# Attention into a gated MLP: two loads brought forward on the DMA queue, and one transposition moved to another PSUM bank

## The chip, the cores and the metric

The kernel runs on one core of a Trainium2 chip. The metric is device time in microseconds for one execution. The engines named below are TensorE (PE, with its weight loads as PEld), VectorE (DVE), ScalarE (ACT), GpSimd (POOL) and SyncE (SP). POOL and SP also issue DMA transfers.

## The reference

```python
# q, k, v: (8, 12, 448, 64); x: (3584, 768); w_gate, w_val: (768, 1536); w_out: (1536, 768)
scores = scale * np.matmul(q, k.transpose(0, 1, 3, 2))
attn = np.exp(scores - max); attn = attn / (sum + 1e-09)
attn_out = np.matmul(attn, v)
x = attn_out.transpose(0, 2, 1, 3).reshape(B * S, H * D)
g = x @ w_gate
silu = g * (1.0 / (1.0 + np.exp(-g)))
return (silu * (x @ w_val)) @ w_out
```

Eight sequences of 448 positions and twelve heads go through softmax attention; the joined heads go through a gated MLP. Inputs and output are float32.

## The kernel before

**Tiles.** The 96 heads are worked on as 48 pairs, six pairs to a sequence. The 3,584 tokens of the MLP are eight blocks of alternately 384 and 512 tokens (`block`, L573). In the MLP, `ffn1_steps` (L488) makes the gate and value products (L493) of one 128-wide slice of the hidden dimension, applies tanh on ACT (L511) and two products on DVE (t at L516, hts at L519); `ffn2_steps` (L526) multiplies by the output weights (L544) and stores through ACT (L551). The output weights are two halves of columns, wo 0 and wo 1 (1,152 KB each in fp16). The first block does all its steps with wo 0 before those with wo 1.

**Attention of one pair.** Keys and queries are loaded with a cast to fp16 on POOL's DMA queue (`load_qk16`, L144, queries at L157; from pair 12 on the keys come as two transfers, one for each half of the partitions, at L138). From pair 14 on a buffer of two pairs is filled by two calls: the even pair of the two takes the buffer, the odd one fills its other half. Then the pair is turned so that the head dimension lies on the partitions. Pairs 1 to 10 are turned by TensorE (`turn`, L249, transposes at L258, copied out by DVE at L259). Pair 11 (L217 copies on POOL, transposes on SP's queue at L220 and L224) and all pairs from 12 on (L194, then L196 and L200) are turned by DMA transposes, which need POOL's copies first; the copies write one of three buffers in turn (tag qk16). The scores (L299 up to pair 11, from 12 on L268 and, for the leftover rows of two pairs together, L281) are followed by the exponential on ACT (L307, L289) and the product with V (L325, L333, L362). V comes by POOL's queue too (L168, from pair 12 on L138) and is copied beside a column of ones by DVE (L175).

**PSUM.** Six of the eight banks are three score banks of two, taken in turn by `stile` (L115) through the list `sring`. The other two are the pool `ps_f`, taken in turn by the value product, the output product, the attention accumulators, the turns and, where `gate_small` is set, a gate product. A user waits until the reader of the same bank before it has ended.

**Order.** The order of work is written out by hand: the program order of each engine is the order in which the Python code emits it. Pairs 0 to 5, with the scores of pair 6's first two chunks, follow the string `order` (L682). After that a loop over `plan` (L739) makes visits x = 0, 1, 2, ... Visit 0 has pair 6's chunks 0 and 1 (already scored), visit 1 chunks 2 and 3, visits 2 and 3 pair 7, and from visit 4 on there are three chunks to a visit: pair 8's first chunk is in visit 4, pair 9's in visit 5, pair 10's in visit 6, pair 11's in visit 8, pair 12's in visit 9. A visit scores its chunks, prepares later pairs, does the products with V of finished pairs, and runs a share of the MLP.

**Loads.** Loads are emitted from the table `wq` (L602): entry n is emitted with the second score chunk of pair n in the prologue (L691, pairs 0 to 6) or at the end of the visit that pair n enters (L777). Items are "qk" (first pair, number of calls' pairs; two if left out), "V" (three pairs), "g" and "v" (a quarter of the gate or value weights), and "o" (a half of the output weights). In addition, when pair n enters a visit, `prep` is emitted for pair n + 3 or n + 4 (L755; pair 11 in visit 4, pairs 12 and 13 in visit 5, pair 14 in visit 6, pair 15 in visit 8), then the keys and queries of pair n + LA with LA = 6 (L759), then V of pair n + 3 from pair 12 on (L761). Before the change, visit 4 therefore loads pair 14, visit 5 pair 15, V of pair 12 and, by entry 9 of the table, wo 1. Entry 6 (V of pairs 9 to 11, and wo 0) is emitted in the prologue, with the second chunk of pair 6.

Of the kernel before, what the change touches and what calls it, by code (L numbers as in the profile page):

```python
# [20 lines left out]
LA = 6  # L21
RB = 5
FIRST = 6
# [14 lines left out]
def kernel(  # L38
# [19 lines left out]
    NPAIR = B * NHP  # L58
# [56 lines left out]
    def stile():  # L115
        sring.append(sring.pop(0))
        return sbanks[sring[-1]]

    def dummy(n, w=512):
        wp = ps_f.tile([128, 512], FP32, tag="f", name="wp")  # L120
        for _ in range(n):
            nc.tensor.matmul(wp[:, 0:w], lhsT=warm[:, 0:128], rhs=warm[:, 0:w], start=True, stop=True)
# [67 lines left out]
    def prep_quad(pr):  # L190
        rq, rk = raw[pr]
        qk16 = attp.tile([128, 2, NC, 2, D], FP16, tag="qk16", name="qk16", bufs=3)
        for dst, src in ((qk16[:, 0], rk), (qk16[0:P, 1], rq)):
            nc.gpsimd.tensor_copy(dst.rearrange("p c h d -> p h c d"), src)  # L194
        qkT[pr] = attp.tile([128, NC * 128 + S], FP16, tag="qkT", name="qkT", bufs=QB)
        nc.sync.dma_start_transpose(  # L196
            qkT[pr][:, 0 : NC * 128].rearrange("p (c q) -> p c q", q=128),
            qk16[:, 0].rearrange("p c h d -> p (c h d)"),
        )
        nc.sync.dma_start_transpose(  # L200
            qkT[pr][:, NC * 128 :].rearrange("p (c q) -> p c q", q=P),
            qk16[0:P, 1].rearrange("p c h d -> p (c h d)"),
        )

    def prep(pr):
        if pr >= QUAD:
            return prep_quad(pr)
        rq, rk = raw[pr]
        if pr == 0 or pr >= NPE:
            qk16 = attp.tile([128, 2, NC, 2, D], FP16, tag="qk16", name="qk16", bufs=3)[0:P]  # L210
            for t, src in enumerate((rq, rk)):
                dst = qk16[:, 1 - t].rearrange("p c h d -> p h c d")
                if pr == 0:
                    nc.vector.tensor_copy(dst[:, 0], src[:, 0])
                    nc.scalar.activation(dst[:, 1], src[:, 1], AF.Copy)
                else:
                    nc.gpsimd.tensor_copy(dst, src)  # L217
        qkT[pr] = attp.tile([128, 2 * S + D], FP16, tag="qkT", name="qkT", bufs=QB)
        if pr >= NPE:
            nc.sync.dma_start_transpose(  # L220
                qkT[pr][:, 0 : 2 * S].rearrange("p (c q) -> p c q", q=P),
                qk16.rearrange("p t c h d -> p (t c h d)"),
            )
            nc.sync.dma_start_transpose(  # L224
                qkT[pr][:, 2 * S :].rearrange("p (c q) -> p c q", c=1),
                qk16[0:D, 1, 0].rearrange("p h d -> p (h d)"),
            )
            return None

        def turn0():  # L230
            for t in range(2):
                tp = stile()
                for c in range(NC):
                    for hx in range(2):
                        nc.tensor.matmul(
                            tp[ts(hx, 64), c // 2, ds(c % 2 * P, P)],
                            lhsT=qk16[:, 1 - t, c, hx],
                            rhs=ident[0:P, 0:P],
                            start=True,
                            stop=True,  # L240
                        )
                dst = qkT[pr][:, ts(1 - t, S)].rearrange("p (a x) -> p a x", a=2)
                nc.vector.tensor_copy(dst[:, 0], tp[:, 0, 0 : 2 * P])
                nc.scalar.activation(dst[:, 1], tp[:, 1, 0 : 2 * P], AF.Copy)
                if t == 0:
                    dummy(1, 256)
                    nc.vector.tensor_copy(qkT[pr][:, 2 * S :], tp[:, 0, 0:D])

        def turn():  # L249
            if pr < FIRST + 2:  # L250
                tp = stile()[:, 0].bitcast(FP16)
            else:
                tp = ps_f.tile([128, 1024], FP16, tag="f", name="tp")
            for i in range(2 * NC + 1):
                t, c = (1 - i // NC, i % NC) if i < 2 * NC else (0, 0)
                for hx in range(2):
                    src = raw[pr][t][:, hx, c, :]
                    nc.tensor.transpose(tp[ts(hx, 64), ts(i, P)], src, ident[0:P, 0:P])  # L258
            nc.vector.tensor_copy(qkT[pr][:], tp[:, 0 : 2 * S + D])  # L259

        return turn if pr else turn0
# [31 lines left out]
    def qk(pr, c):  # L293
        if pr >= QUAD:
            return qk_quad(pr, c)
        t = qkT[pr]
        s = stile()
        for hx in range(2):
            nc.tensor.matmul(  # L299
                s[:, hx, 0:S],  # L300
                lhsT=t[ts(hx, 64), c * P : c * P + 128],
                rhs=t[ts(hx, 64), ds(S + (1 - hx) * D, S)],
                start=True,
                stop=True,
            )
        e = Es[pr % NE][:, ds(c * EB, 16)].rearrange("p (h b) x -> p h (b x)", h=2)
        nc.scalar.activation(e[:, :, 0:S], s[0:P, :, 0:S], AF.Exp, scale=sm_scale)  # L307
# [271 lines left out]
    with tc.manual_schedule():  # L579
# [5 lines left out]
        for vo in Vts:  # L585
# [18 lines left out]
            1: [("V", 2), ("qk", 8, 1), ("g", 1), ("v", 1)],  # L604
            3: [("qk", 9, 1), ("qk", 10), ("g", 2), ("v", 2)],
            4: [("g", 3), ("v", 3), ("qk", 12)],
            6: [("V", 3), ("o", 0)],
            9: [("o", 1)],
        }

        def emit(item):
# [127 lines left out]
        for x, (chunks, todo) in enumerate(plan):  # L739
            quads = [u for u in chunks if u[0] >= QUAD and u[1] == RU]  # L740
            for pr, c in quads + [u for u in chunks if u not in quads]:
                if x > 0:
                    qk(pr, c)
            for _, p0 in todo:
                if p0 >= QUAD:
                    pv_piece(p0, RU)
            end = min([y for y in adds if y > x] + [len(plan) + 1])
            if x == 0:
                add_block(0, end)
            early = [p0 for p0 in vcopies.get(x, []) if p0 < QUAD]  # L750
            for p0 in early:
                copy_v(p0)
            entered = [pr for pr, c in chunks if c == 0]
            for pr in entered:
                lead = [pr + 3] if pr + 3 < QUAD else [pr + 3, pr + 4] if pr + 3 == QUAD else [pr + 4]  # L755
                for p in lead:
                    if NPE <= p < NPAIR:
                        prep(p)
                if 14 <= pr + LA < NPAIR:  # L759
                    load_qk16(pr + LA, 1)  # L760
                if 12 <= pr + 3 < NPAIR:  # L761
                    load_v(pr + 3)
            for pr, c in chunks:
                if c == 2 and pr < NPE - 2:
                    prep(pr + 2)()
            if x in adds and x > 0:
                add_block(adds[x], end - x, x)
            for _, p0 in todo:
                pv(p0)
                if p0 < XPE:  # L770
                    turns.append(p0)
                else:
                    turn_x(p0)
            for p0 in vcopies.get(x, []):
                if p0 not in early:
                    copy_v(p0)
            for pr in entered:  # L777
                for w in wq.pop(pr, []):
                    emit(w)
            bare = not todo and bool(chunks)  # L780
            if x == 0:
                carry = left() / end
                for fb in range(3):
                    gate_small[0] = fb == 2
                    carry -= run_fv()
            elif adds[max(y for y in adds if y <= x)] < 2:
                if bare and oq and not fvq:
                    carry -= run_o()
                elif bare:
                    gate_small[0] = True  # L790
                carry = run_budget(left() / (end - x) + carry)
            else:
                nf, no = steps.pop(0) if steps else (0, 0)
                if bare and no:
                    run_o()
                    no -= 1
                elif bare:
                    gate_small[0] = True
                for y in range(nf):
                    if fvq:  # L800
                        run_fv()
                for _ in range(no):
                    run_o()
            if x == 1:
                turn_rests(0)
            while turns:
                turn_x(turns.pop(0))
            if XPE - 1 in [p0 for _, p0 in todo]:
                turn_rests(1)
# [39 lines left out]
```

## Time and profile before

| what | value |
|---|---|
| median of 3 runs | 453.12 us (452.09 to 453.83) |
| the profiled execution | 452.5 us |
| its span (first to last instruction) | 450.7 us |
| mean granted TensorE clock | 0.995 |
| POOL's DMA queue (q0) | 46,832 packets, 24.56 MB, 48.7% of 16 engines' span |
| SP's DMA queue (q1: transposes and stores) | 61,520 packets, 24.66 MB, 28.7% |
| wo, two issues | 1,152 KB each, 14.3 us from issue to landing (median) |

The profile counts the time of an engine's instructions as busy and gives, for every idle stretch, the instruction or transfer that ended it. Times in the trace are microseconds from the start of the span. Sizes of loads are those written (fp16). "Landing" is the time from the issue of a transfer to its completion.

### The profile page before, as it was taken

Reading aid. Unit: us, or ns where it says so; the run is one execution under the profiler, and the core shown is the slowest. Engines: PE = TensorE matmul, PEld = TensorE weight load, DVE = VectorE, ACT = ScalarE, POOL = GpSimd, SP = SyncE. Lnnn points to the kernel's source line nnn. Section 1 sums busy time; section 2 is a strip of 40 time slices with the busy share of each in tenths; the row PEclk is TensorE's granted clock in tenths of the full one; section 3 lists DMA queues with packets and bytes.
Section 4 is the critical chain, followed back from the end, with each engine's and each line's share of the span. In section 5 each row is a group of like instructions: output and inputs, shape, how many; then the busy total and the mean of one; then the engine's idle time right before and its main releaser. Section 6 shows DMA issues by size and latency. Waiting matters only on the chain.

```text
span 450.7 us, 10033 instructions
## 1 busy us (share of the span) xinstructions
PE 438.9 (97%) x4025; PEld 246.7 (55%) x4025; DVE 199.9 (44%) x447; ACT 225.0 (50%) x332; POOL 180.4 (40%) x299
## 2 busy tenths in 40 slices
PE   8999998999999999999999999999999999999996
PEld 3665664544456566554556556554455656644464
DVE  4756551365564344343454434344444434045400
ACT  6975765546553654455536365455454651222222
POOL 8655735997875364336461366423000000000000
PEclk9999999899999999999999999999999999999999
DMA  9999999999997699975975688945131211200033
GB/s 140 176 200 201 197 172 174 154 201 160 134 142 94 108 140 120 125 119 69 125 109 101 111 128 106 155 78 97 32 79 47 50 43 23 79 27 0 0 107 105
DMA packets 108494, 49.90 MB, mean 111 GB/s; under 512 B 60832, under 2 KB 104992, under 8 KB 108448
## 3 DMA queue, kind: packets, MB, share of 16 engines
q0 software_dynamic: 46832, 24.56, 48.7%
q1 hardware_dynamic: 61520, 24.66, 28.7%
q8 instruction: 31, 0.51, 0.5%
q14 instruction: 15, 0.12, 0.1%
q10 hardware_dynamic: 96, 0.05, 0.0%
HBM read 49.55 MB, written 11.01 MB: 134 GB/s over the span
## 4 chain that ended last, share of the span: by engine, by line
PE 78%; DMA 14%; DVE 3%; POOL 2%; issue 1%; ACT 1%; DVEq 0%; ACTq 0%; POOLq 0%
PE op L544 23%; PE s L493 21%; PE vp L493 19%; PE acc L362 8%; DMA wv<-in_moe_w_val_dram 5%; PE s L268 4%; DMA k<-in_k_dram 3%; DMA wo<-in_moe_w_out_dram 3%; DMA wg<-in_moe_w_gate_dram 2%; DVE hts L519 1%; DVE t L516 1%; ACT sg L511 1%; PE s L281 1%; DMA vraw<-in_v_dram 1%; POOL k L157 1%
## 5 line engine op out<-in xcount | busy, mean ns | idle before, releaser
L493 PE MATMUL vp<-X,wv 128*128 128x512 f16 (+1 forms) x564 | 122.4, 353 | 0.1
L544 PE MATMUL op<-wo,hts 128*128 128x384 f16 (+1 forms) x684 | 116.6, 325 | 2.6 <-DMA wo<-in_moe_w_out_dram 2.2
L493 PE MATMUL s<-X,wg 128*128 128x512 f16 (+1 forms) x534 | 116.4, 354 | 0.0
L289 ACT ACTIVATE E<-s 128x896 f16<-128x896 f32 x126 | 106.5, 921 | 13.6 <-PE s L268 8.7
L516 DVE SCALAR_TENSOR_TENSOR t<-sg,s 128x512 f32<-128x512 f32 (+1 forms) x91 | 56.7, 623 | 107.3 <-ACT sg L511 107.3
L511 ACT ACTIVATE sg<-s 128x512 f32<-128x512 f32 (+1 forms) x91 | 49.9, 549 | 93.6 <-PE s L493 91.1
L544 PEld LDWEIGHTS <-hts 128*128 128x128 f16 x684 | 66.1, 98 | 48.3 <-issue 2.9
L493 PEld LDWEIGHTS <-wv 128*128 128x128 f16 x564 | 55.1, 98 | 52.1 <-issue 0.4
L551 ACT ACTIVATE osb<-op 128x384 f32<-128x384 f32 (+1 forms) x57 | 27.7, 486 | 103.7 <-PE op L544 102.3
L493 PEld LDWEIGHTS <-wg 128*128 128x128 f16 x564 | 52.4, 98 | 44.9 <-issue 0.7
L519 DVE SCALAR_TENSOR_TENSOR hts<-t,vp 128x512 f16<-128x512 f32 (+1 forms) x94 | 58.5, 622 | 10.2 <-DVE t L516 0.5
L194 POOL COPY qk<-k 128x512 f16<-128x512 f16 x36 | 22.8, 632 | 99.3 <-DMA qkT<-qk 97.5
L138 POOL DMA_DIRECT2D vraw<-in_v_dram x72 | 43.8, 627 | 9.8 <-DMA wo<-in_moe_w_out_dram 6.5
L138 POOL DMA_DIRECT2D k<-in_k_dram x70 | 42.3, 616 | 7.0 <-DMA wo<-in_moe_w_out_dram 4.8
L362 PEld LDWEIGHTS <-E 128*128 128x128 f16 (+1 forms) x1152 | 37.2, 96 | 13.1 <-issue 7.6
L307 ACT ACTIVATE E<-s 112x896 f16<-112x896 f32 x48 | 40.7, 917 | 6.6 <-PE s L299 5.8
L403 DVE RECIPROCAL R<-acc 128x4 f32<-128x4 f32 x68 | 12.0, 177 | 70.9 <-PE acc L362 70.9
L362 PE MATMUL acc<-vo,E 128*128 128x65 f16 (+1 forms) x1088 | 40.8, 193 | 2.2 <-DVE hts L519 1.9
L157 POOL DMA_DIRECT2D q<-in_q_dram x44 | 30.1, 683 | 5.3 <-PE acc L333 1.8
L404 DVE TENSOR_TENSOR xt<-acc,R 128x256 f16<-128x256 f32 x68 | 28.8, 424 | 2.3
L268 PE MATMUL s<-qkT 64*128 64x448 f16 x216 | 28.3, 355 | 0.0
L194 POOL COPY qk<-q 112x512 f16<-112x512 f16 x36 | 23.1, 642 | 0.0
(70 smaller groups left out, 208.6 us busy)
## 6 DMA issues: line engine op xcount, KB each, us to landing
vraw<-in_v_dram POOLq DMA_DIRECT2D x72, 64.0 KB, 4.5
q<-in_q_dram POOLq DMA_DIRECT2D x41, 112.0 KB, 3.8
k<-in_k_dram POOLq DMA_DIRECT2D x68, 64.0 KB, 4.5
wg<-in_moe_w_gate_dram POOLq DMA_DIRECT2D x8, 288.0 KB, 9.8
wv<-in_moe_w_val_dram POOLq DMA_DIRECT2D x8, 288.0 KB, 10.2
wo<-in_moe_w_out_dram POOLq DMA_DIRECT2D x2, 1152.0 KB, 14.3
out_dram<-osb SPq DMA_DIRECT2D x8, 288.0 KB, 3.7
out_dram<-osb SPq DMA_DIRECT2D x6, 336.0 KB, 2.8
```

The lines of the kernel that those rows point to most:

```text
L138: eng.dma_start(dst[ts(s, 64)], rows)
L157: nc.gpsimd.dma_start(dst[0:P, ds(h0, 2 * n)], flat.rearrange("h (p c) d -> p h (c d)", c=NC))
L194: nc.gpsimd.tensor_copy(dst.rearrange("p c h d -> p h c d"), src)
L268: nc.tensor.matmul(s[:, hx, 0:S], lhsT=t[ts(hx, 64), ts(c + low(pr, hx), 128)], rhs=t[ts(hx, 64), ds(NC * 128, S)], start=True, stop=True,)
L289: nc.scalar.activation(e[:, 0 : 2 * S].rearrange("p (h q) -> p h q", h=2), s[:, :, 0:S], AF.Exp, scale=sm_scale)
L307: nc.scalar.activation(e[:, :, 0:S], s[0:P, :, 0:S], AF.Exp, scale=sm_scale)
L362: nc.tensor.matmul(accs[pr][0][hx][:, ts(j, D + 1)], lhsT=e[rows, ds(hx * S + j * 128, 128)], rhs=Vts[pr % NV][rows, hx, col, 0 : D + 1], ...
L493: nc.tensor.matmul(dst[:, 0:n], lhsT=wslice(kind, fb, cb), rhs=X[kk][:, cb, ds(c0, n)], start=(cb == 0), stop=(cb == NCB - 1),)
L511: nc.scalar.activation(sg[:, 0:n], gp[:, 0:n], AF.Tanh, scale=0.5)
L516: nc.vector.scalar_tensor_tensor(t1[:, 0:n], sg[:, 0:n], 1.0, gp[:, 0:n], ALU.add, ALU.mult)
L519: nc.vector.scalar_tensor_tensor(hts[:, fb, 0:n], t1[:, 0:n], 0.5 * HS, vp[:, 0:n], ALU.mult, ALU.mult)
L544: nc.tensor.matmul(op[:, 0:w], lhsT=hts[:, fb, ts(ch, 128)], rhs=wo[oh][:, fb, ds(m0 - oh * OH, w)], start=(fb == 0), stop=(fb == NFB - 1),)
```

## The change

Three edits. Pair 14's keys and queries are loaded by entry 6 of the table, between V of pairs 9 to 11 and wo 0, instead of in visit 4; the loop over visits loads by itself only from pair 15 on. wo 1 is emitted by entry 7, in visit 2, instead of entry 9, in visit 5; on POOL, which has no other instruction between, it follows wo 0 directly. And pair 8, which was turned in a `ps_f` bank, is turned in a score bank, as pairs 1 to 7 are.

```diff
@@ def turn() in prep
-            if pr < FIRST + 2:
+            if pr < FIRST + 3:
                 tp = stile()[:, 0].bitcast(FP16)
             else:
                 tp = ps_f.tile([128, 1024], FP16, tag="f", name="tp")
@@ the table wq
             4: [("g", 3), ("v", 3), ("qk", 12)],
-            6: [("V", 3), ("o", 0)],
-            9: [("o", 1)],
+            6: [("V", 3), ("qk", 14, 1), ("o", 0)],
+            7: [("o", 1)],
@@ the loop over visits
-                if 14 <= pr + LA < NPAIR:
+                if 15 <= pr + LA < NPAIR:
                     load_qk16(pr + LA, 1)
```

FIRST is 6.

## The prediction

> **What bounds the kernel now.** I read the engine row first, then who TensorE (PE) waited for, then the region of the longest wait: clock, instructions in order of time, and the DMA issues with their landings. PE is busy for 438.9 of the 450.7 us. Its end is the kernel's end, so a microsecond changes the time only if PE idles less or runs at a better clock.
>
> ```profile
> span 450.7 us, 10033 instructions
> PE 438.9 (97%) x4025; PEld 246.7 (55%) x4025; DVE 199.9 (44%) x447; ACT 225.0 (50%) x332; POOL 180.4 (40%) x299
> PE op L544 <- DMA wo<-in_moe_w_out_dram: 2.2, 1, 2.2
> PE tp L258 <- DVE t L516: 0.7, 1, 0.7
> ```
>
> The third line is PE's longest wait: once, 2.2 us, for the second half of the output weights. The fourth, 0.7 us, is the turn of pair 8. These two are what the change can touch. Next, the table by stretches around the long wait (length, busy time of PE, PEld, DVE, ACT, POOL, then the granted clock):
>
> ```profile
> 70.00:74.50 4.50, 4.50 (x59) 2.50 (x58) 1.21 (x2) 4.50 (x7) 2.33 (x4) 1.00 1.36 161
> 74.50:77.00 2.50, 0.28 (x7) 0.14 (x4) 1.03 (x3) 1.24 (x2) 0.00 (x0) 1.00 1.32 187
> 77.00:79.00 2.00, 2.00 (x10) 1.06 (x9) 0.00 (x0) 0.00 (x0) 1.29 (x3) 0.70 1.36 183
> 79.00:80.00 1.00, 1.00 (x6) 0.49 (x5) 0.00 (x0) 0.00 (x0) 1.00 (x2) 0.50 1.35 185
> 80.00:81.00 1.00, 1.00 (x18) 0.62 (x17) 0.60 (x2) 0.49 (x1) 1.00 (x3) 0.50 1.41 189
> ```
>
> After the idle 2.2 us the clock falls to 0.70 and 0.50 until about 81 us. So the wait has a second bill. The 12 output matmuls after it take 2.96 us from start to next start, against 1.95 for such a dozen in the chain of waits: 1.0 lost. The transposes, rests and scores behind them take 0.45, 0.47 and 0.98, against 0.27, 0.31 and 0.58 for the same elsewhere: 0.7 more. Wait and slow clock together: 2.2 + 1.7 = 3.9 us.
>
> Why is that weight late? POOL's instructions in order of time:
>
> ```profile
> 44.82 0.78 POOL L168 DMA_DIRECT2D vraw<-in_v_dram  x1 [1.18 <-DVE t L516]
> 46.92 1.04 POOL L188 DMA_DIRECT2D wo<-in_moe_w_out_dram  x1 [1.33 <-issue]
> 47.96 0.62 POOL L217 COPY qk<-q 112x512 f16<-112x512 f16 x1
> ...
> 52.70 0.62 POOL L194 COPY qk<-k 128x512 f16<-128x512 f16 x1 [1.74 <-DMA k<-in_k_dram]
> ...
> 63.84 0.60 POOL L138 DMA_DIRECT2D vraw<-in_v_dram  x1 [6.47 <-DMA wo<-in_moe_w_out_dram]
> 64.79 1.03 POOL L188 DMA_DIRECT2D wo<-in_moe_w_out_dram  x1 [0.35 <-DMA k<-in_k_dram]
> 65.82 0.62 POOL L194 COPY qk<-k 128x512 f16<-128x512 f16 x1
> ```
>
> The loads behave as if **eight are in flight**: an issue waits until the eighth one before it has landed. Counted from the first weight issue at 46.92 (it lands at 46.92 + 16.6 = 63.5), the loads are three for pair 14, three for pair 15, one for V of pair 12, and the eighth is the vraw at 63.84, which starts 0.3 us after that landing. The wo of 64.79 follows in the same way 0.3 us after the queries of pair 14 (49.06 + 15.4), and the earlier issues that wait fit too. It lands at 64.79 + 12.0 = 76.8; PE starts at 76.88.
>
> **The change, part by part.**
>
> *Pair 8's turn in a score bank.* No instruction is added. PE reaches it at 33.7 and starts at 34.35, when DVE has read the gate (34.31). The score bank it gets instead is the one whose reader, the second hts product of the block, ends at 33.84: the turn can start 0.5 us sooner. But the ring then moves on by one, and pair 7's second score gets the bank that the exponentials of pair 6 free at 35.32 (33.59 + 1.73). Before, both scores ran from 35.32 to 35.81; one can now run ahead. Gain 0.2 us; bounds 0 and 0.5.
>
> *The order on POOL.* New order: V of pairs 9 to 11 (unchanged, 44.82), three loads of pair 14, wo 0, wo 1, then the two copies of pair 11, the four of pairs 12 and 13, the loads of pair 15 and V of 12, the copies of 14, and so on. By the rule of eight: pair 14's loads wait for loads landing at 45.7, 47.1 and 48.6; wo 0 for one at 50.1, so about 50.4; wo 1 for the queries of pair 12, landing at 51.3, so about 51.7 with 1.0 us of issue. Pair 11's copies start at 52.7 instead of 47.96: **4.7 us later**. Those of 12 and 13 start at 53.8 instead of 52.70, and all six queue on SP behind pair 11's two transposes.
>
> *What lands when.* The queue of the loads is never empty here. Between 49 and 53 us it moves some 390 packets of 512 bytes per us; the weights' 768-byte packets go at 260 per us alone (69 to 70.5 us) and at 188 beside transposes, which get as many packets (54 to 60 us). Pair 14's 480 packets cost 1.2 us ahead of wo 0, whose 1,536 packets then run alone for some 3.5 us, as the transposes start later; it lands at about 63, and PE wants it at 65.82: free. wo 1 follows directly: 1,536 at 188 is 8.2 us, landing at 70.5 to 72.5. PE wants it at 74.65. The wait and its slow clock go: **-3.9 us**.
>
> *What is late instead.* Pair 11's transposes were issued at 49.16 and 50.56 and landed at 58.7 and 59.2. PE read them at 64.06, a slack of 4.9. 4.7 us later they land at 63.4 and 63.9, and PE is there at 63.85: the slack is used up. I charge 0.4 us. Pairs 12 and 13 landed at 65.2 and 68.7 and were needed at 70.19 and 72.72. The transposes are one stream; it ran from 53.2 to 67.9 and would run from 57.9. Pair 12 (960 packets at about 188) ends near 69.5, in time; pair 13, once wo 1 has left, at 73.0 to 73.7, 0.8 late. New waits: 0.4 + 0.8 = **1.2 us**. Below nothing is excluded, as a later input makes nothing earlier. The upper end: of the six transposes issued from 49 to 59 us the slowest took 12.1 us where I use 9.5, 2.6 more, and there were two gaps of about 1 us (60.5 and 71.6) in which both queues nearly stood. Pair 11 could thus cost 0.4 + 2.6 + 0.9 = 3.9 us.
>
> *Other edits.* Pair 14's copies use the buffer that pair 11's transposes free, so start near 64.3 (before: 65.82); its transposes come behind 13's and land near 77.5, needed at about 78.3. Pair 15's copies wait behind loads that wait for wo 1 (eighth before) and start at 73 to 75 instead of 69.94; they land near 81.5, needed at about 84.5. V of 12 lands near 73.6 and DVE wants it at 75.47. All are covered, by 0.8 to 3 us. If that cover goes, each costs PE its lateness.
>
> [...] The row is the clock: an idle of 2.2 us was followed by 0.70 and 0.50, while the idle 0.7 us at 34.35 left the stretch 33 to 36 us at 1.00. [...]
>
> **Sum.** -0.2 - 3.9 + 1.2 = -2.9 us. The profiled execution took 452.5 us (450.7 of span and 1.8 around it), so 449.6; the median shown is 453.12, 0.6 above it, so **450.2 us**, 0.64% faster.
>
> **Rivals.**
> 1. *No new wait*: the transposes of 11 and 13 come a little earlier, since until 57.9 nothing shares the engines with wo 0. For it: slack of 4.9 against a delay of 4.7. Against it: nothing else runs ahead of them. 453.1 - 4.1 = 449.0.
> 2. *The wait is swapped*: pairs 11 and 13 cost 2 to 4 us together, some of it at the slow clock. For it: four inputs in a row with under 1 us of cover, and the gaps of the queues. Price: with 3.5 us of waits, 453.1 - 4.1 + 3.5 = 452.5, no change.
> 3. *Slower: pair 11 is turned too late.* Place: POOL between wo 0 and the copies of pair 11. At wo 1's issue loads of 4,736 rows would be in flight. Before, the most was 4,320, at the first wo, which sat 1.33 us for no reason shown. If that is the queue's room, wo 1 waits for the keys of pair 12 (52.6), 1.2 us more. With the slowest transpose and a gap, pair 11 lands at 63.9 + 1.2 + 2.6 + 0.9 = 68.6: 4.7 us of idle and 1.7 of slow clock, 6.4 - 4.1 = +2.3, 455.4. Against it: it needs all three. It breaks even at a landing of 66.2 and loses 0.5% from 68.6 on.
> 4. *The change doesn't do what it says*: wo 1 still lands behind PE's 74.65, as all loads share the same engines. Against it: only 736 packets of 512 bytes (pair 15 and V of 12) pass from ahead of it to behind it, 1.9 to 2.9 us, but POOL's blocked stretch also goes. 452.5.
>
> **Chances.** Forecast 0.50, rival 1 0.12, rival 2 0.18, rival 3 0.15, rival 4 0.05. About 0.5% (2.3 us) is what a measurement here can tell from no change. The forecast's own range, with waits of 0.2 to 2.5 us, is 449.2 to 451.5, and a fifth of it lies within 0.5%. Faster 0.40 + 0.12 = 0.52; within 0.10 + 0.18 + 0.05 = 0.33; slower 0.15. The range reaches from rival 1 less 0.4 for the spread of runs to just short of rival 3: 448.6 to 455.0.
>
> **What would show it.** Right: no wait of L544 for wo; the clock at 1.00 from 74 to 82 us; wo 1 issued by 53 us and landed before 73; copies of pair 11 near 52.7; new PE waits at L299 near 64 and L281 near 73 of about a microsecond in all; the turn of pair 8 waiting 0.2 us. Wrong: wo 1 issued after 54 us, a PE wait of over 2 us at pair 11, or a low clock anywhere between 60 and 85 us.

## The result and the profile after

The changed kernel takes 453.87 us (median of 6 runs, 453.32 to 454.77) against 452.94 for the kernel before on the same chip: ratio 1.002, 95% interval 0.9999 to 1.0041. That is no change that can be measured here; 450.2 was forecast. The profiled execution took 454.77 us, the longest of the six, with a span of 453.0.

Who PE waited for, in the changed kernel (us in total, times, longest):

```profile
span 453.0 us, 10034 instructions
PE s L299 <- DMA qkT<-qk: 3.0, 1, 3.0
PE s L281 <- DMA qkT<-qk: 1.2, 1, 1.2
PE s L299 <- ACT E L307: 0.3, 1, 0.3
PE s L268 <- DVE X L466: 0.3, 1, 0.3
PE s L258 <- DVE hts L519: 0.2, 1, 0.2
```

The wait for wo is gone, and pair 8's turn waits 0.2 us instead of 0.7. In their place PE waits 3.0 us for the turned keys and queries of pair 11 (L299) and 1.2 us for those of pair 13 (L281). PE's own work is the same: 438.9 us busy in both.

PE's own row shows the two waits (start, length, what it does, idle time before it and what ended that):

```profile
67.02 1.29 PE L299 MATMUL s<-qkT 64*128 64x448 f16 x6 [3.02 <-DMA qkT<-qk]
78.67 0.38 PE L281 MATMUL s<-qkT 64*64 64x448 f16 x3 [1.17 <-DMA qkT<-qk]
```

The table by stretches (start and end, length, busy time of PE, PEld, DVE, ACT and POOL, granted clock) shows the second bill, the slow clock after a long wait, again, some ten microseconds earlier than before:

```profile
64.00:66.00 2.00, 0.00 (x1) 0.00 (x0) 1.06 (x3) 0.00 (x0) 0.00 (x0) 1.00 1.30 191
66.00:68.00 2.00, 0.98 (x6) 0.33 (x6) 0.00 (x0) 0.39 (x1) 0.97 (x2) 0.77 1.28 192
68.00:70.00 2.00, 2.00 (x34) 1.75 (x33) 0.00 (x0) 2.00 (x3) 1.41 (x3) 0.50 1.28 190
70.00:72.00 2.00, 2.00 (x15) 1.17 (x13) 0.83 (x2) 0.14 (x1) 0.00 (x0) 0.88 1.47 169
72.00:74.00 2.00, 2.00 (x15) 1.20 (x13) 0.00 (x0) 0.49 (x1) 0.59 (x1) 1.00 1.39 168
```

PE stands still from 64 to 67 us and then runs at a granted clock of 0.50 until about 70.5. All six timed executions of the changed kernel show a mean granted clock of 0.995 or 0.996, so the slow stretch is in each of them. The scores, the products with V and the first 24 output products after the wait take 1.23, 1.75 and 4.14 us; before they took 0.80, 0.96 and 3.90. That is 1.5 us.

POOL's order shows where pair 11's copies (L217) went:

```profile
52.76 2.05 POOL L188 DMA_DIRECT2D wo<-in_moe_w_out_dram  x2 [2.26 <-issue]
54.80 0.63 POOL L217 COPY qk<-q 112x512 f16<-112x512 f16 x1
55.35 0.63 POOL L217 COPY qk<-k 112x512 f16<-112x512 f16 x1
55.90 0.62 POOL L194 COPY qk<-k 128x512 f16<-128x512 f16 x1
```

They start at 54.80, 6.8 us later than before (47.96). Pair 11's transposes are issued at 56.00 and 57.58 and land at 66.4 and 66.9; PE is at the scores at 64.0 and starts them at 67.02.

The account of the two profiled executions: gone are 2.2 us of wait, 1.7 of slow clock and 0.5 at the turn; new are waits of 3.0, 1.2, 0.3 and 0.3 and 1.5 of slow clock. 6.3 - 4.4 = 1.9 of the 2.3 us by which the spans differ. The medians differ by 0.9 only: this execution is the longest of its six, and about 1 us of its waits is not the change's, as shown below.

### The profile page after: what moved, and what is told of

Read it like the earlier page. It is cut to its first block, busy times and chain, and to the rows that moved or that the text cites. A ratio compares the mean times of both kernels' runs of the same rounds, so it can differ in the third digit from the quotient of the medians.

```text
span 453.0 us, 10034 instructions
## 1 busy us (share of the span) xinstructions
PE 438.9 (97%) x4025; PEld 247.0 (55%) x4025; DVE 199.0 (44%) x447; ACT 224.8 (50%) x332; POOL 180.6 (40%) x299
## 4 chain that ended last, share of the span: by engine, by line
PE 77%; DMA 12%; POOL 4%; DVE 3%; issue 2%; ACT 1%; SPq 0%; DVEq 0%; ACTq 0%; POOLq 0%
PE op L544 23%; PE s L493 21%; PE vp L493 19%; PE acc L362 8%; DMA qkT<-qk 5%; PE s L268 4%; DMA vraw<-in_v_dram 3%; DMA wv<-in_moe_w_val_dram 3%; DMA k<-in_k_dram 2%; DVE hts L519 1%; DVE t L516 1%; PE s L281 1%; ACT sg L511 1%; POOL q L157 1%; POOL k L157 1%
## 5 line engine op out<-in xcount | busy, mean ns | idle before, releaser
L544 PEld LDWEIGHTS <-hts 128*128 128x128 f16 x684 | 66.0, 98 | 45.7 <-issue 2.4
L519 DVE SCALAR_TENSOR_TENSOR hts<-t,vp 128x512 f16<-128x512 f32 (+1 forms) x94 | 58.5, 623 | 10.2 <-DVE t L516 0.5
L403 DVE RECIPROCAL R<-acc 128x4 f32<-128x4 f32 x68 | 12.1, 178 | 71.3 <-PE acc L362 71.3
L268 PE MATMUL s<-qkT 64*128 64x448 f16 x216 | 28.1, 353 | 0.3 <-DVE X L466 0.3
```

Source lines behind the costliest of these rows:

```text
L268: nc.tensor.matmul(s[:, hx, 0:S], lhsT=t[ts(hx, 64), ts(c + low(pr, hx), 128)], rhs=t[ts(hx, 64), ds(NC * 128, S)], start=True, stop=True,)
L519: nc.vector.scalar_tensor_tensor(hts[:, fb, 0:n], t1[:, 0:n], 0.5 * HS, vp[:, 0:n], ALU.mult, ALU.mult)
L544: nc.tensor.matmul(op[:, 0:w], lhsT=hts[:, fb, ts(ch, 128)], rhs=wo[oh][:, fb, ds(m0 - oh * OH, w)], start=(fb == 0), stop=(fb == NFB - 1),)
```

## The experiments

Theory A: the new waits come from POOL's order alone. Pair 11's copies stand behind the issues that were brought forward; everything behind them, on POOL and on SP, is late with them. Theory B: wo 1's packets, which now move while the transposes of pairs 11 to 13 do, take the DMA engines from them. Rival C: the shifted ring of score banks costs waits later. Rival D: the slow clock does not come from the idle time, or costs nothing. Each kernel was timed beside the kernel before, on the same chip; ratios are to that (452.64 us for e1 to e4, 453.11 for e5 to e8). Intervals are 95%.

For B it matters when wo 1's packets move. In the profiles of the kernel before and of the changed kernel all 219 transfers that POOL issues land in the order of their issue, so I take wo 1's packets to move between the landing of the load before it and its own (in e3 8.3 us for its 1,536 packets).

**Only the turn of pair 8** (e1_turn_only)

```diff
-            if pr < FIRST + 2:
+            if pr < FIRST + 3:
```

> The kernel before with only pair 8 turned in a score bank. Theory A (the new waits of the changed kernel come from POOL's order alone): PE starts the turn 0.4 us sooner, keeps 0.1 to 0.2 us of it, and still waits 2.2 us for wo 1 with the slow clock after it; 0.0 to -0.3 us, about 452.8, not to be told from no change. Rival C (the shifted ring of score banks costs waits later on): new waits of L299, L268 or L493 for ACT, and over 453.5.

Measured: 452.96 against 452.64, ratio 1.0002 (0.9983 to 1.0020). The turn waits 0.2 us, pair 7's second score 0.3 (for ACT, the one new wait that the shifted ring brings, and forecast), the wait for wo is 2.4. No other wait for ACT is new, and the time is under C's 453.5. This part of the change is worth nothing that can be measured.

**Only pair 14's loads** (e2_pair14_only)

```diff
-            6: [("V", 3), ("o", 0)],
+            6: [("V", 3), ("qk", 14, 1), ("o", 0)],
-                if 14 <= pr + LA < NPAIR:
+                if 15 <= pr + LA < NPAIR:
```

> The kernel before with only pair 14's keys and queries moved ahead of wo 0. Theory A: pair 11's copies on POOL stand behind three more issues, which wait for loads landing at 47 to 50 us, so they start at 52 to 53.5 instead of 47.96; pair 11's scores wait 0 to 1.5 us. POOL no longer stops from 57 to 64 us, since the first weight is no longer the eighth before V of pair 12, and wo 1 goes out near 58 instead of 64.79 and lands near 74.5: the wait for it shrinks from 2.2 to under 0.7 us. Sum -1 to -3 us, 450 to 452. Theory B (wo 1's packets beside the transposes are what delays pairs 11 and 13): here wo 1 comes late, so pairs 11 and 13 wait nothing, and 449.5 to 450.5.

Measured: 453.42, ratio 1.0009 (0.9988 to 1.0031); 450 to 452 was expected of A, 449.5 to 450.5 of B. wo 1 comes late, as in the kernel before (landing at 76.5), and yet pairs 11 and 13 are late. For pair 11 B is wrong: its transposes had landed by 65.6 us, and wo 1's packets moved only from 67.6 on. Pair 13's transposes landed at 72.5 and 76.3, beside wo 1, so for pair 13 this run does not decide. A has the place right and the size wrong again, and it did not expect the wait for pair 13. PE's waits:

```profile
PE s L299 <- DMA qkT<-qk: 1.9, 1, 1.9
PE s L281 <- DMA qkT<-qk: 1.7, 1, 1.7
```

The copies of pair 11 start at 52.54, within what was expected, but their transposes take 11.1 and 10.2 us to land, not 9.5 and 8.6. The two waits, 3.6 us together, left the clock at 1.00 in this execution (seven of the twelve timed ones have 0.996, so there the slow clock came); they cost about what the wait for wo 1 and its slow clock had cost (3.9), so the time stays.

**Only wo 1** (e3_wo1_only)

```diff
-            9: [("o", 1)],
+            7: [("o", 1)],
```

> The kernel before with only wo 1 moved to visit 2, directly behind wo 0. Theory A: wo 1's issue waits for nothing long, so pair 11's copies start only 1 us later (near 49) and pair 11 is not waited for; but the second transfer of V of pair 12 must now wait for wo 1's landing (it is the eighth after it), near 72, and pair 14's copies stand behind it: they start near 72.5 instead of 65.8 and PE waits 3 to 6 us for pair 14 near 79 us. No wait for wo 1. Sum 0 to +3.5 us, 452.5 to 456. Theory B: wo 1's packets run beside the transposes of pairs 11 to 13, so PE waits 3 us for pair 11 and 1 us for pair 13 as in the changed kernel, and nothing for pair 14.

Measured: 452.38, ratio 0.9992 (0.9972 to 1.0011), just under the 452.5 to 456 that A expected; the profiled execution, 453.78, is one of the longest of its twelve. Pair 11's copies start at 48.66, and neither pair 11 nor pair 13 is waited for, though wo 1's packets move from 62.9 to 71.1, beside the transposes of pairs 12 and 13 (landing at 63.6 to 71.6): against B for pair 13. POOL's next instructions show the wait that takes the place:

```profile
63.40 0.60 POOL L138 DMA_DIRECT2D vraw<-in_v_dram  x1 [6.59 <-DMA wo<-in_moe_w_out_dram]
71.42 0.59 POOL L138 DMA_DIRECT2D vraw<-in_v_dram  x1 [7.43 <-DMA wo<-in_moe_w_out_dram]
72.49 0.61 POOL L194 COPY qk<-k 128x512 f16<-128x512 f16 x1 [0.47 <-DMA k<-in_k_dram]
```

The two transfers of V of pair 12 are the eighth issues after wo 0 and wo 1, and each waits for its weight to land. Pair 14's copies, behind them, start at 72.49, and PE waits 3.9 us for pair 14, with a slow clock from 79.1 to 85.9. So the eight in flight are seen here too (starts 0.5 and 0.3 us after landings at 62.9 and 71.1), and either half of the change by itself moves the wait to another pair.

**wo 1 in visit 4, pair 14 where it was** (e4_wo1_visit4)

```diff
-            9: [("o", 1)],
+            8: [("o", 1)],
```

> The kernel before with wo 1 emitted by entry 8 instead of 9: behind pair 11's copies and pair 14's loads, ahead of the copies of 12 and 13. Theory A: pair 11's copies start near 48 as before, those of 12 and 13 near 53 as before; wo 1 goes out near 52 and lands near 73; no wait for wo 1, none for pairs 11 to 13 above 0.3 us, pair 15's copies come 4 to 6 us later within their slack. Sum -3 to -4 us, 449 to 450. Theory B: wo 1's packets run beside the transposes of pairs 12 and 13, so PE waits 1 us or more for pair 13 or 14, and 451 or more.

Measured: **449.97, ratio 0.9937 (0.9912 to 0.9961)**: faster than both kernels, by a little less than the 3 to 4 us that A expected. POOL makes pair 11's copies as early as in the kernel before, and wo 1 goes out 5 us after them:

```profile
47.38 0.62 POOL L217 COPY qk<-q 112x512 f16<-112x512 f16 x1
47.93 0.62 POOL L217 COPY qk<-k 112x512 f16<-112x512 f16 x1
...
52.15 1.03 POOL L188 DMA_DIRECT2D wo<-in_moe_w_out_dram  x1 [0.63 <-DMA q<-in_q_dram]
53.38 0.61 POOL L194 COPY qk<-k 128x512 f16<-128x512 f16 x1 [0.19 <-DMA k<-in_k_dram]
```

wo 1 lands at 74.1. PE waits for neither wo nor pair 11 and 0.2 us for pair 13; a wait of 1.1 us for DVE's copy of the leftover rows (L268 for L466) is new, and the clock stays at 1.00 from 62 to 82 us. wo 1's packets move from 65.7 to 74.1, beside pair 13's transposes (landing at 67.3 and 69.8), here too: B is out. The gain that the change was forecast to bring is there, once nothing PE needs soon stands behind the weights.

**The changed kernel with pair 11's copies put first** (e5_after_copies11_first; the diff in part)

```diff
-            6: [("V", 3), ("qk", 14, 1), ("o", 0)],
+            6: [("c", 11), ("V", 3), ("qk", 14, 1), ("o", 0)],
...
+    def copies(pr):
+        copied[pr] = attp.tile([128, 2, NC, 2, D], FP16, tag="qk16", name="qk16", bufs=3)[0:P]
+        for t, src in enumerate(raw[pr]):
+            nc.gpsimd.tensor_copy(copied[pr][:, 1 - t].rearrange("p c h d -> p h c d"), src)
...
+        if pr in copied:
+            qk16 = copied[pr]
```

> The changed kernel with one thing put back: POOL makes pair 11's two copies before V of pairs 9 to 11, so ahead of pair 14's loads and both weights. Both weights and pair 14's loads stay where the change put them. Theory A (the loss is POOL's order: pair 11's copies, and through SP's queue those of 12 and 13, stand behind two weight issues): the copies start near 44 us, pair 11 lands near 55, the 3.0 us wait at 64 and the slow clock after it go, the wait for pair 13 shrinks to 0 to 0.8 us, no wait for wo 1; 3.5 to 5 us under the changed kernel, 449 to 450.5. Theory B (wo 1's packets beside the transposes delay them): pairs 12 and 13 are still late by 1 to 3 us, and 451 or more.

Measured: **450.07 against 453.11, ratio 0.994 (0.9917 to 0.9963)**. Everything the change moved stays where the change put it; only two copies, 1.2 us of POOL's time, stand elsewhere. POOL's order and PE's one wait for turned keys and queries (lines count from this kernel's own text; the copies are now L210):

```profile
43.81 0.62 POOL L210 COPY qk<-q 112x512 f16<-112x512 f16 x1
44.36 0.62 POOL L210 COPY qk<-k 112x512 f16<-112x512 f16 x1
...
52.58 2.06 POOL L188 DMA_DIRECT2D wo<-in_moe_w_out_dram  x2 [2.94 <-issue]
55.36 0.62 POOL L194 COPY qk<-k 128x512 f16<-128x512 f16 x1 [0.72 <-DMA k<-in_k_dram]
```

```profile
PE s L290 <- DMA qkT<-qk: 0.3, 1, 0.3
```

The copies start at 43.81, pair 11 lands at 54.5 and 55.2, and the waits of 3.0 and 1.2 us become 0 and 0.3. wo is not waited for, and wo 1's packets (64.8 to 74.1) still move beside pair 13's transposes. Both weights are issued as late as in the changed kernel (52.58 against 52.76). This undoes the whole loss by its supposed cause alone, so the cause is shown.

**Filling the wait for wo 1 in the kernel before** (e6_before_warm; ten matmuls on zeros are added)

```diff
+            if first and oh == 1 and ch == 0:
+                dummy(10)
             for m0, w in parts:
```

> The kernel before with ten more 512-wide matmuls on zeros (a scratch bank, 2.15 us at full clock) on PE directly ahead of the first product with wo 1, where it waits 2.2 us. Nothing else is changed. Theory A (the idle time itself brings the slow clock, 1.7 us): the wait shrinks to 0 to 0.4 us, the granted clock stays at 1.00 from 74 to 82 us, and the time falls by 1.0 to 1.7 us, to 451 to 451.6. Rival D (the clock falls for another reason, or the fall costs PE nothing that it would not have waited for anyway): no change, 452.4 to 453.2.

Measured: 451.90, ratio 0.9979 (0.9964 to 0.9994). In the profiled execution wo 1 landed late enough to leave 0.9 us of wait, where 0 to 0.4 was expected, but the clock did not fall:

```profile
74.00:76.00 2.00, 2.00 (x26) 1.14 (x23) 1.03 (x3) 1.61 (x2) 0.00 (x0) 1.00 1.29 191
76.00:78.00 2.00, 1.12 (x7) 0.42 (x5) 0.00 (x0) 0.00 (x0) 0.29 (x1) 1.00 1.35 183
78.00:80.00 2.00, 2.00 (x26) 1.26 (x23) 0.12 (x1) 0.29 (x1) 1.41 (x3) 1.00 1.36 184
```

The output products run at full clock straight after the wait (1.94 us for the dozen). The time fell by 0.2%, about 1.0 us, at the lower end of the fall that A expected. All twelve executions have a granted clock of 0.999 or 1.000. Of the 55 timed executions of the kernel before in these experiments 44 have 0.992 to 0.996 and 11 have 0.998 to 1.000; the 11 are shorter by 1.2 and 2.1 us in the medians of the two sets (those beside e1 to e4 and beside e5 to e8), though a shorter wait may be part of that. D is wrong: with 0.9 us of idle time instead of 2.2 the slow clock is gone, so it is a bill of the idle time. The matmuls on zeros also take one turn of the `ps_f` banks; no new wait in this profile is over 0.4 us.

**The faster version with the turn as well** (e7_visit4_turn; both diffs, of e4 and of e1)

> The kernel with wo 1 in visit 4 (449.97) and pair 8 turned in a score bank as well. Theory A: 0.0 to 0.3 us less, 449.7 to 450.0; pair 8's turn waits 0.2 instead of 0.7 us, and the second score of pair 7 waits 0.3. Rival C (the shifted ring costs later): 450.3 or more.

Measured: 450.14, ratio 0.9944 (0.9925 to 0.9963), against 0.9937 for the version without. The turn's bank makes no difference that can be told; C's threshold was not reached.

**Filling the wait for pair 11 in the changed kernel** (e8_after_warm; fourteen matmuls on zeros are added)

```diff
+            if x == 8:
+                dummy(14)
```

> The changed kernel with fourteen more 512-wide matmuls on zeros (3.0 us) on PE directly ahead of pair 11's scores, where it waits 3.0 us. Theory A (waits of 3.0 and 1.2 us and a slow clock of 1.5 us are what ate the 3.9 us gained): the wait at pair 11 shrinks to 0 to 0.8 us, the clock stays at 1.00, and the time falls by 0.8 to 1.5 us, to 452.4 to 453.1. Rival D: no change, 453.5 to 454.2.

Measured: 453.39, ratio 1.0003 (0.9984 to 1.0022); the changed kernel itself had 1.0020. The clock stays at 1.00 from 62 to 86 us and pair 13 is waited for by 0.3 us; all twelve executions have a granted clock of 0.999 or 1.000, where all six of the changed kernel have 0.995 or 0.996. But the filling was too long:

```profile
64.13 3.18 PE L122 MATMUL wp<-warm 128*128 128x512 f16 x14 [0.74 <-DVE hts L519]
67.24 0.74 PE L299 MATMUL s<-qkT 64*128 64x448 f16 x6
```

The added matmuls first waited 0.7 us for their bank and ended at 67.24. Pair 11 had landed at 65.0 and 65.5, and PE was there at 63.4: in this execution the wait to fill was 2.1 us, not 3.0, and the filling itself held PE up for 1.7. The step from the changed kernel is in A's direction but smaller than forecast and inside both intervals: inconclusive in the time, clear in the clock.

## Why the prediction was wrong, step by step

**The bound, the wait and its slow clock: right.** The wait for wo 1 went, as forecast, and was priced at 3.9 us with its slow clock. The versions e4 and e5, which remove it without the loss, are 0.63% (0.39 to 0.88) and 0.60% (0.37 to 0.83) faster, 2.9 and 2.7 us; they add small waits of their own (1.1 us at L466 in e4; 0.4, 0.3, 0.3 and 0.3 in e5, less 0.5 at the turn), so 3.9 fits within the intervals. The profiles show the slow clock after idle times of 2.2 us (kernel before), 2.4 (e1), 3.0 (changed kernel) and 3.9 (e3), and none after 1.95 and 1.7 (e2), 1.2 (changed kernel) and 0.9 (e6), one profile for most of these. In the kernel before the granted clock is 0.50 from 77.9 to 81.1 us, in the changed kernel from 67.1 to 70.4.

**The turn: right in the trace, too small for the time.** It waits 0.5 us less and pair 7's second score 0.3 more, the 0.2 that was forecast; the time shows 0.0 within 0.2%.

**The rule of eight: right in the runs**, with one constant missed. In the profiles of the two kernels none of the 219 transfers that POOL issues starts before the eighth one before it has landed; those that wait for it start 0.3 to 0.6 us after. The first wo issue starts 1.2 to 1.3 us after, in all ten profiles (46.92 after 45.7 before, 52.76 after 51.5 in the changed kernel). It does so with 4,320 rows (packets of 512 or 768 bytes) in flight in the one and 3,200 in the other, and in e3 wo 1 followed wo 0 without a wait with 5,472 in flight, so rival 3's reason for it, the queue's room, is wrong. What the extra 1.0 us is stays open.

**"What is late instead": the step that failed.** Its chain was right link by link; its term for pair 11 was far too small. It let pair 11's transposes land at 63.4 and 63.9 and charged 0.4 us; they landed at 66.4 and 66.9, and PE waited 3.0, with 1.5 us of slow clock behind it that the sum had at nothing. The 3 us are two terms:
- 2.1 us: the copies start at 54.80, not at 52.7. Some 0.7 of it is the first wo issue, 1.0 later than the rule gives, less the 0.3 that the forecast had left between the two wo issues. The other 1.4 is the load that wo 0 waits for, which landed at 51.46 instead of 50.1: the load queue of that execution was 1.0 us late from 23 us on, before the change could act (the second gate weight of the second quarter was issued at 23.01 against 22.00). That 1.0 is not the change's, and it fits with the profiled execution being the longest of its six.
- 0.7 to 0.9 us: the transposes took 10.4 and 9.3 us from issue to landing where 9.5 and 8.6 were carried over.

Run e8 has the same order on POOL without the late queue. Its copies start at 53.03, 0.3 from the forecast, but its transposes take 10.8 and 9.8 us, and pair 11 lands at 65.5, 2.1 us after PE got there. So what is left there of the error is mostly the transposes' time. In e2 they took 11.1 and 10.2. In these three a gap of both queues falls into that time (at 61.0 in the changed kernel, 59.5 in e8); in the kernel before it came at 60.5, after pair 11 had landed (58.7 and 59.2).

This is the general mistake: a duration was carried to another time as if it belonged to the transfer. The text had the gaps and the 12.1 us in its bounds (up to 3.9 us for pair 11), but set the likeliest value at the least of them, where a slack of 4.9 us had been eaten to 0.2. Two of its own signs of being wrong came: a wait of over 2 us at pair 11 and a low clock between 60 and 85 us.

**The price of a late input jumps.** The forecast charged lateness one for one. In these profiles the slow clock came on top (1.5 us in the changed kernel) after the waits of 2.2 us and more and after none of 1.95 and less, so the sum is not smooth: in the profiled executions e2 with 1.9 and 1.7 us of waits paid 3.6, the changed kernel with 3.0 and 1.2 paid 5.7.

**Pair 13: right in place; the size is luck.** 0.8 us was forecast and 1.2 measured, but pair 13 landed at 78.6, not 73.7, 4.9 us later, and PE came 4.4 us later itself (77.12 against 72.72), held up by pair 11. The two errors nearly cancel. **Pairs 14, 15 and V of 12: covered**, as forecast.

The outcome is rival 2's, no change, at a higher price: 5.7 us at pairs 11 and 13 with the slow clock, where it had 3.5. The place is rival 3's (POOL between wo 0 and pair 11's copies), without rival 3's reason. That loss and gain come out so nearly equal is chance.

## What to carry to other kernels

Before a DMA issue is moved ahead on a queue, list what it is moved past on the issuing engine: here two copies of 0.6 us each, behind weights that wait for older loads, decided 3.6 us (ratio 1.002 for the changed kernel, 0.994 for e5). Put a big early load behind the small work that another engine needs soon, not in front: wo 1 one place later in the table than the change put it, with pair 14's loads left where they were, gave 0.63%, the gain that was forecast. And when a step eats a slack down to a few tenths of a microsecond, charge the spread of the transfer, not its one duration, and the clock on top where the idle time may pass what was seen to leave it at 1.00 (1.95 us here; 2.2 us did not).

## What the runs showed of the hardware

**A gap of both DMA queues after a packet of the instruction queue (q8, as the profile names it), in all ten profiles.** Such a packet falls between 58.9 and 60.2 us, and within 2 us of it both data queues together drop from about 190 packets in half a microsecond to 9 to 99 (in the kernel before from 180 at 59.5 to 50 at 61.0, in the changed kernel from 170 at 60.5 to 99 at 61.0). Where the packet came early (58.9, e8) the gap did too (59.5), where it came late (60.2, e7) the gap came at 61.0. In the kernel before the next is at 70.9 with a gap at 72.0, in the changed kernel at 75.7 with the long gap shown here. First the queues of the changed kernel from 75.5 to 76.0 us, then the stretches after (last column GB/s):

```profile
q1 hardware_dynamic: 264, 0.07, 119.6%
q8 instruction: 1, 0.02, 25.1%
q0 software_dynamic: 29, 0.01, 18.3%
```

```profile
77.00:77.50 0.50, 0.50 (x3) 0.11 (x2) 0.00 (x0) 0.50 (x2) 0.50 (x2) 1.00 3.70 51
77.50:78.00 0.50, 0.00 (x0) 0.00 (x0) 0.00 (x0) 0.22 (x1) 0.50 (x2) 1.00 0.32 7
78.00:78.50 0.50, 0.00 (x0) 0.00 (x0) 0.00 (x0) 0.00 (x0) 0.50 (x2) 1.00 0.10 10
```

The rate falls from 51 to 7 GB/s, and pair 13's transpose, the one PE waits 1.2 us for, lands at 78.6 just behind it. That the packet causes the gap is not shown: no run moved it alone, and the packet near 48 us of the kernel before, when no transposes were in flight, was followed by no gap; nor was the one at 70.5 us in e3, where the transposes were just ending.

**A DMA transpose's time to landing differs with the time of its issue**: 7.9 to 13.3 us for those issued from 48 to 73 us, 3.3 to 6.7 us for those issued between 76 and 87 us, when the loads too land soon (3.1 to 5.9 us after their issue, in the two kernels). From 61.5 to 70.0 us of the changed kernel, with both queues busy, they move packets one for one (1,627 and 1,622; 94 and 92 from 63.5 to 64.0).
